# A delta-net recurrence and its feed-forward layer on one Trainium2 core: the first chunk goes from values to feed-forward by units of 128 rows, beta comes in two loads, three chunks' loads stand on two queues, and the order of all instructions is a new one

## The chip, the cores and the metric

The kernel runs on one core of one Trainium2 chip. The core has five engines, each with its own queue of instructions: PE (matmuls and transposes, with PEld for the loading of their weights), DVE (vector), ACT (activation functions and copies with a scale), POOL (a second vector engine, which also issues some DMAs) and SP (here it only issues DMAs). Engines wait for each other by semaphores. A result of PE lands in PSUM, of which there are eight banks; everything else is in SBUF.

The metric is the time of one execution on the device in microseconds (us). Before the change it was 254.03 us, the median of three runs (253.86, 254.03 and 255.42).

## The reference

Eight heads of four batches run a recurrence over 768 steps with a 48 x 48 state each. Their output, 3072 tokens of 384 numbers, goes through a feed-forward layer of width 2048.

```python
# q, k, v: [4, 8, 768, 48]   beta: [4, 8, 768]
k_n = k / (np.linalg.norm(k, axis=-1, keepdims=True) + 1e-06)
for t in range(S):
    y[:, :, t] = np.einsum('bhd,bhde->bhe', q[:, :, t], state)
    v_old = np.einsum('bhde,bhd->bhe', state, kt)
    state = state + bt[:, :, :, None] * np.einsum('bhd,bhe->bhde', kt, vt - v_old)
x = y.transpose(0, 2, 1, 3).reshape(3072, 384)
h = x @ w_in                                   # 384 x 2048
g = 0.5 * h * (1.0 + np.tanh(c * (h + 0.044715 * h * h * h)))
out = g @ w_out                                # 2048 x 384
```

## The kernel before

**Tiling.** The 768 steps are cut into 12 chunks of 64. Inside a chunk the recurrence is solved as a triangular system, so that nearly all work is matmuls; only the state goes from chunk to chunk. A chunk holds 256 tokens. It is worked on as two *units* of 128 rows (two batches x 64 steps on the 128 partitions, with the eight heads side by side); unit u belongs to chunk u // 2. Names carry the chunk or the unit: `up3.5` is block 3 of chunk 5, `B4.2` the first unit of chunk 1.

**Stages of a chunk**, with the line of the kernel before:

- *load* (L463): k, q and v, each in four DMAs of 96 KB; only chunk 0's k comes in eight of 48 KB, four for each unit (`k0x0`, `k0x1`). Chunk 0's k may be issued by ACT or SP, all others by SP.
- *norms* (L486): `sq` squares k, `sum` adds, `pow`, `eps` and `inv` give 1/(|k| + 1e-6).
- *prep* (L505): normalised k and q in bf16 (`tok`); their turned form `kT`, made either by PE transposes (`Tk`, `Tq`, `T`, all L540, and a copy) or by one DMA transpose (`turn`, SP); products of keys with keys and with queries (L564), copied as `dn` and `wq`; `vb`, the bf16 copy of v.
- *leaf* (L627): inverts the blocks on the diagonal, 8 x 8 each. `F` and `L` are matmuls, then a chain of 12 small steps follows in one of two forms: on DVE straight in PSUM (`xm`, `xa`, L655 and L658), or after a copy of the PSUM bank (`Lc`) on POOL or DVE in SBUF (`ym`, `ya`). `xb` (L669) multiplies by beta.
- *scale* (L592): `xe` spreads `xb` into the tile `zt`; `KZ` (L609) and `kz`; the scaled key products `GM` (L620); `lw` (L623).
- *invert* (L672): doubles the inverted blocks in two levels: `X10`, `X11` (affine selects, L682), then `A4`, `rt4`, `B4`, `bde4`, and `A5`, `rt5`, `B5`, `be5` (matmuls L692 and L697). The result of `B4` goes to the tile `bd` either directly (`bde40`, `bde41`) or by a copy (`xi`) and POOL (`bdc`).
- *chain* (L725): `V` (values, L759), `K` and `Q` (products with the state, L752), `R` (copy to `rs`), `U` (L773), `Un` (copy to `us`), `S` (state, L782), `Sn` (copy to `st`), `O` (output, L795), `On` (copy to `xo`), then the output is turned to `xT` by PE (`X`, L807, and the copy `xT`) or by a DMA transpose (`turnx`, L812). Chunk 0 has no state before it, so it has no `K` and `Q`.
- *mlp* (L816): 16 `up` (L824, three 256-column matmuls each), a `gelu` on ACT for each four of them (L828), 2 x 4 `down` (L835, four 384-column matmuls each), copies `Z` to `ob`, and the output DMAs.

Around these there are constants, presets of tiles, the activation-table loads `tabS` and `tabG`, the four loads of the weights on POOL's queue (`w1.0`, `w1.1`, `w2.0`, `w2.1`: half a matrix each, 768 KB in bf16; L476), beta (L428) and `fill` (L426): a 128 x 512 matmul on zeros whose result nobody reads.

**Beta.** `beta` is loaded in four DMAs: steps of chunk 0 apart from the other eleven chunks. Each part is turned (`betaT`), negated (`betaN`, four pieces), split into two bf16 summands (`betaH`, `betaL`) and spread over the partitions (`betaS`, `betaC`).

**What sets the order.** Every operation is declared once, with what it reads and writes:

```python
A(PE, op("U"), umat, reads=inv + [rbn], alloc=(ps("U"), 2), mode="m", mm=16)
A(EV, op("Un"), lambda e, P: copy(e, ub[:, :, :, :, :].rearrange("p x y g d -> p x (y g d)"), banks(P(ps("U")))),
  frees=[ps("U")], writes=[ubn])
```

Which engine executes it, in which place, in which PSUM bank and in which of its alternative forms is written in one long text, `ORDER`: `Un.0:a` puts `Un` of chunk 0 into ACT's queue at that place (p, a, d, g, s for PE, ACT, DVE, POOL, SP), `U.0@0` puts `U` on PE and its result in bank 0. An alternative that is not named there is not executed. Each engine executes its operations in just that order. The program derives the semaphore waits from the declarations, so an operation that waits holds up all that stands behind it on its engine. Chunks overlap widely: while PE does the `up` and `down` of one chunk, the other engines prepare the next two or three.

## Time and profile before

| What | Value |
|---|---|
| median of three runs | 254.03 us (253.86 to 255.42) |
| profiled execution, from its first to its last instruction | 254.7 us |
| mean granted clock of PE in it | 0.966 of full speed |
| instructions | 12256 |
| PE, busy | 226.0 us (89%), 5500 instructions |
| DVE, busy | 185.8 us (73%), 445 instructions |
| ACT, busy | 157.4 us (62%), 244 instructions |
| POOL, busy | 130.1 us (51%), 159 instructions |
| moved by DMA | 28.25 MB, mean 111 GB/s |
| `up` (L824), 576 matmuls of 128x256 | 76.8 us |
| `down` (L835), 384 matmuls of 128x384 | 72.7 us |

The profile is of one execution, by the hardware profiler. Busy times of engines overlap each other, and so do PE's matmuls and its weight loads (PEld); a share of busy time is a mean over the whole span and says nothing about one stretch of it. In rows of groups `out<-in` names the tiles, then come the operation's shape, its count, the busy time, the mean of one in ns, and the idle time of the engine just in front of them with what ended it. The granted clock is the share of its full speed at which PE was allowed to run. Records of matmuls end where a model says, so that a busy PE isn't always PE at its peak.

### The profile page before, as it was taken

To read this page: it belongs to the slowest core of one execution; us is meant where nothing else is said; L and a number is where in the kernel's file an instruction comes from. 1 tells how busy PE (TensorE), PEld (TensorE's weight loads), DVE (VectorE), ACT (ScalarE), POOL (GpSimd) and SP (SyncE) were. 2 spreads that over 40 slices of the span, in tenths; PEclk is the share of its full clock that TensorE was granted. 3 is DMA by queue.
4 is the path that set the end of the run, shared out by engine and by line. 5 is a ranking of instruction groups with operands and counts; after the bars stand their busy time and mean duration, and the time that the engine had idled before them with its cause. 6 is when DMAs were issued, how large, how long until landed. Compare 5 with 4: busy or idle time off the path is not lost.

```text
span 254.7 us, 12256 instructions
## 1 busy us (share of the span) xinstructions
PE 226.0 (89%) x5500; PEld 178.3 (70%) x5502; DVE 185.8 (73%) x445; ACT 157.4 (62%) x244; POOL 130.1 (51%) x159
## 2 busy tenths in 40 slices
...
GB/s 103 165 144 118 184 162 95 165 127 117 128 130 105 112 126 124 135 165 147 119 146 167 100 36 131 147 153 130 56 93 167 62 49 4 33 68 64 3 93 62
DMA packets 104532, 28.25 MB, mean 111 GB/s; under 512 B 98592, under 2 KB 103712, under 8 KB 104480
## 3 DMA queue, kind: packets, MB, share of 16 engines
...
q14 instruction: 9, 0.07, 0.1%
...
## 4 chain that ended last, share of the span: by engine, by line
PE 73%; DVE 15%; ACT 4%; DMA 2%; ACTq 2%; issue 2%; SPq 1%; POOL 0%
PE ps L835 24%; PE ps L824 22%; PE ps L692 5%; PE ps L620 3%; PE ps L752 3%; PE ps L773 2%; DMA vraw<-in_v_dram 2%; PE ps L697 2%; PE ps L564 2%; DVE lw L623 2%; DVE xl L658 2%; PE ps L633 2%; PE ps L759 2%; DVE ps L655 2%; PE ps L609 1%
## 5 line engine op out<-in xcount | busy, mean ns | idle before, releaser
L824 PE MATMUL ps<-xT,W 128*128 128x256 bf16 x576 | 76.8, 277 | 0.4 <-DVE xl L658 0.4
L835 PE MATMUL ps<-W,gT 128*128 128x384 bf16 x384 | 72.7, 326 | 0.0
L828 ACT ACTIVATE gT<-ps 128x1024 bf16<-128x1024 f32 x48 | 48.4, 1022 | 26.4 <-PE ps L824 25.8
L824 PEld LDWEIGHTS ps<-xT,W 128*128 128x128 bf16 x576 | 52.2, 99 | 9.3 <-DVE xl L658 0.5
L835 PEld LDWEIGHTS ps<-W,gT 128*128 128x128 bf16 x384 | 34.0, 97 | 18.2
L682 POOL TENSOR_SCALAR_AFFINE_SELECT bd<-lw 64x512 bf16<-64x512 bf16 x34 | 22.6, 667 | 37.7 <-DVE lw L623 28.6
L704 DVE TENSOR_TENSOR rl<-ps,two 128x384 bf16<-128x384 f32 (+1 forms) x48 | 22.9, 484 | 9.7 <-PE ps L692 9.5
L623 DVE CAST_PREDICATED lw<-mlw,ps 128x832 bf16<-128x832 uint16 x24 | 24.3, 1018 | 6.8 <-PE ps L620 6.5
L499 POOL TENSOR_TENSOR nrm<-nrm,half 128x16 f32<-128x16 f32 x9 | 26.6, 2956 | 2.8 <-DVE nrm L497 2.7
L343 ACT ACTIVATE bd<-ps 32x256 bf16<-32x256 f32 (+1 forms) x40 | 16.8, 428 | 8.2 <-PE ps L692 4.4
L692 PEld LDWEIGHTS ps<-lw,bd 128*128 128x128 bf16 x384 | 15.5, 98 | 4.2 <-POOL bd L682 1.2
L692 PE MATMUL ps<-lw,bd 128*128 128x32 bf16 (+1 forms) x384 | 17.2, 183 | 1.2 <-POOL bd L682 1.1
L658 DVE TENSOR_TENSOR xl<-ps,xl 128x96 bf16<-128x96 f32 (+4 forms) x72 | 16.0, 228 | 2.0
L655 DVE TENSOR_TENSOR ps<-ps,xl 128x64 f32<-128x64 f32 (+5 forms) x72 | 15.6, 221 | 2.0 <-PE ps L649 0.5
L343 ACT ACTIVATE ob<-ps 128x384 f32<-128x384 f32 x17 | 8.3, 490 | 14.0 <-PE ps L835 14.0
L722 POOL COPY bd<-xi 64x256 f32<-64x256 f32 x20 | 8.0, 401 | 16.4 <-ACT xi L343 8.5
L540 PE MATMUL ps<-ident,tok 128*128 128x128 bf16 x80 | 7.8, 246 | 8.1 <-POOL tok L531 3.8
L531 POOL TENSOR_TENSOR tok<-kraw,nrm 128x384 bf16<-128x384 f32 x9 | 8.5, 945 | 12.7 <-DVE bsb L349 5.6
L349 ACT ACTIVATE kT<-ps 128x512 bf16<-128x512 f32 x18 | 10.4, 596 | 6.4 <-PE ps L609 6.4
L343 ACT ACTIVATE dn<-ps 128x512 bf16<-128x512 f32 x18 | 10.4, 593 | 5.3 <-PE ps L564 5.3
L620 PE MATMUL ps<-kT 48*64 48x56 bf16 (+1 forms) x768 | 11.1, 196 | 2.8 <-ACT kT L349 1.4
L599 POOL TENSOR_TENSOR zt<-xb,blk 128x2048 bf16<-128x2048 bf16 x3 | 10.9, 3642 | 4.1 <-DVE xb L669 3.9
...
## 6 DMA issues: line engine op xcount, KB each, us to landing
...
W<-in_moe_w_in_dram POOLq DMA_DIRECT2D x2, 768.0 KB, 8.8
W<-in_moe_w_out_dram POOLq DMA_DIRECT2D x2, 768.0 KB, 9.6
kraw<-in_k_dram ACTq DMA_DIRECT2D x7, 48.0 KB, 3.3
...
```

The lines of the kernel that those rows point to most:

```text
L343: return e.activation(out, in_, ACT.Copy) if e is nc.scalar else e.tensor_copy(out, in_)
L499: if e is nc.scalar else e.tensor_tensor(nr[:, 1, hx], nr[:, 0, hx], half[:, hx], ALU.pow), reads=[nrn, "half"] + ["one"] * (c < ROOTS),
L620: ins = e.matmul(P(ps("GM"))[hf(a), o_ + c0:o_ + c1], kT[s][r, y, g, hf(a)], kT[s][r, z, g, C * a + c0:C * a + c1])
L623: A(("dve",), op("lw"), lambda e, P: e.copy_predicated(lw[m][:, :, 0:LW - LB], mlw[:, :, :].rearrange("p w t -> p (w t)")[:, 16:16 + LW - ...
L655: A(("dve",), f"xm{m}.{c}", lambda e, P, m=m, w=w, part=part: e.tensor_tensor(part(P), P(f"L.{c}")[:, off[m]:off[m] + 2 * H * w].rearrange ...
L658: A(("dve",), f"xa{m}.{c}", lambda e, P, m=m, part=part: e.tensor_tensor(xl[y][:, :, m + 1:LB], part(P), xl[y][:, :, m + 1:LB], ALU.add), ...
L682: A(("pool", "dve"), op(f"X1{a}"), lambda e, P, src=lw[m][hf(a), :, LW - C:LW], dst=bd[b_][hf(a), :, hf(a)], a=a: e.affine_select(out=dst, ...
L692: ins = e.matmul(P(name)[:, C * h + c0:C * h + c1], bd[b_][:, h, :], rhs[:, h, :])
L704: A(("dve",), op(f"rt{i}"), lambda e, P, i=i, c0=c0, c1=c1, r_=r_: e.tensor_tensor(r_[:, 0:H, c0:c1], P(ps(f"A{i}")).rearrange("p (h t) -> ...
L824: ins = e.matmul(P(ph)[:, 256 * f:256 * f + 256].rearrange("p (x t) -> p x t", x=2), W1[:, j, 128 * (i + f):128 * (i + f) + 128], x_[:, :, ...
L828: A(("act",), f"gelu{i // 4}.{c}", lambda e, P, i=i, ph=ph: e.activation(g_[:, i:i + 4, :], P(ph).rearrange("p (f t) -> p f t", f=4), ACT. ...
L835: ins = e.matmul(P(po)[:, 0:DM], g_[:, f, 128 * b:128 * b + 128], W2[:, f, :], start=(f == 0), stop=(f == FC - 1))
```

## The change

Five things change, and the text `ORDER` is written anew around them.

- **Chunk 0 by units.** From `V` to `xT` chunk 0 is done for each of its two units apart, on half of the columns: `Va`, `Ra`, `Ua`, `Una`, `Oa`, `Ona`, `Xa`, `xTa`, and the same with b. `S` stays whole and waits for both. Its `up` become `upa` and `upb`, 16 of three 128-column matmuls each, with a `gelua` or `gelub` for each eight of them; `down` of a unit reads the gelus of that unit alone. All other chunks stay whole.
- **Beta** comes in two DMAs instead of four, is turned by one group of 12 transposes, negated in four pieces, split once and spread by three `betaS` of four chunks each.
- **Loads**: k, q and v of chunks 0 to 2 may be issued by SP or ACT.
- **Weights**: `w1` no longer waits for chunk 1's k, `w2` no longer for chunk 0's v.
- **Order**, as counts of operations in `ORDER`, before and after: `fill` 2 and 29; units turned by PE (`T`, behind the first two chunks) 6 and 2, by `turn` 14 and 18; chunks whose output is turned by PE 4 and 1 (chunk 0, in halves), by `turnx` 8 and 11; chunks whose leaf chain runs in SBUF (`Lc`, `ym`, `ya`) none and six (0, 5, 7, 8, 9, 11); `bdc` by way of `xi` 24 (for 12 units) and none. `bde4` is then always direct, on ACT or DVE.

```diff
 ORDER (its first lines)
-bdz3:d tmplz:g k0x1.10:a k1.01:s tmpl0:g tmpl1:g bdz5:d k0x1.00:a beta11:s blk1:g ...
...
         def load_beta():
             bv = beta.rearrange("b h s -> (b h) s").rearrange("r (c t) -> r c t", t=C)
-            for z, c0, c1 in (("0", 0, 1), ("1", 1, NC)):
+            for y in range(2):
+                A(("sp", "act"), f"beta{y}", lambda e, P, y=y: e.dma_start(braw[:, :, y, :], bv), writes=[f"braw{y}"], dma="beta")
+            def trans(e, P):
+                for c in range(NC):
+                    ins = e.transpose(P("psb")[:, 32 * c:32 * c + 32], braw[:, c, :, :].rearrange("r x t -> r (x t)"), identf[:, :])
+                return ins
...
+            for i in range(NC // 4):
+                d0, d1, w = 4 * i, 4 * i + 4, 8 * H
...
+                A(PE, f"betaS{i}", own_, reads=["rows", "bh", "bl"], alloc=(f"bc{i}", 1), mode="m", mm=2 * LB)
...
         def load(c):
-                            A(("sp", "act") if c == 0 and n == "k" else SP, f"{n}{c}" + ("" if x is None else f"x{x}") + f".{a}{y}",
+                            A(("sp", "act") if c < 3 else SP, f"{n}{c}" + ("" if x is None else f"x{x}") + f".{a}{y}",
...
                 A(("pool",), f"w1.{i}", lambda e, P, f0=f0: e.dma_start(W1[:, :, f0:f0 + FF // 2], w1v[:, :, f0:f0 + FF // 2]),
-                  reads=["kraw10", "kraw11"], writes=[f"W1{i}"], dma=f"w1{i}")
+                  writes=[f"W1{i}"], dma=f"w1{i}")
                 A(("pool",), f"w2.{i}", lambda e, P, n0=n0: e.dma_start(W2[:, n0:n0 + FC // 2, :], w2v[:, n0:n0 + FC // 2, :]),
-                  reads=["vraw00", "vraw01"], writes=[f"W2{i}"], dma=f"w2{i}")
+                  writes=[f"W2{i}"], dma=f"w2{i}")
...
         def chain(c):
+            if first:
+                for x, n_ in enumerate("ab"):
...
+                    A(PE, pn("V"), vh, reads=[f"zt{us_[x] % NN}", vrn[x]], alloc=(pn("K"), 1), mode="m", mm=8)
+                    A(EV, pn("R"), lambda e, P, x=x, half=half: copy(e, rb[:, :, x, :, :].rearrange("p y g d -> p y (g d)"), half(P, "K")), frees=[pn("K")], writes=[f"{rbn}{x}"])
...
+                    A(PE, pn("U"), uh, reads=inv[2 * x:2 * x + 2] + [f"{rbn}{x}"], alloc=(pn("U"), 1), mode="m", mm=8)
...
+                    A(PE, pn("O"), oh, reads=[f"{ubn}{x}", f"wq{ss[x]}"], alloc=(pn("O"), 2), mode="t", mm=16)
...
+                    A(PE, pn("X"), xh, reads=[f"{xbn}{x}", "ident"], alloc=(pn("X"), 1), mode="m", mm=3)
+                    A(EV, pn("xT"), lambda e, P, x=x, pn=pn: copy(e, xT[0][:, x, :, :].rearrange("p j t -> p (j t)"), P(pn("X")).bitcast(BF16)[:, 0:DM]),
+                      frees=[pn("X")], writes=[f"xT0{x}"])
...
         def mlp(c):
+            if c == 0:
+                for x, n_ in enumerate("ab"):
+                    for i in range(0, FC, 8):
...
+                                for j in range(J):
+                                    ins = e.matmul(P(ph)[:, 128 * f:128 * f + 128], W1[:, j, 128 * (i + f):128 * (i + f) + 128], x_[:, x, j, :], start=(j == 0), stop=(j == J - 1))
...
+                        A(("act",), f"gelu{n_}{i // 8}.{c}", lambda e, P, i=i, ph=ph, x=x: e.activation(
+                            g_[:, i:i + 8, 128 * x:128 * x + 128], P(ph).rearrange("p (f t) -> p f t", f=8), ACT.Gelu_apprx_tanh),
...
-                    A(PE, f"down{b}{i // 4}.{c}", down, reads=[f"{gn}.{i // 4}", f"W2{i // 8}"],
+                    A(PE, f"down{b}{i // 4}.{c}", down, reads=[f"{gn}.{i // 4}.{b}", f"W2{i // 8}"],
```

Three places show how the new order stands against the old one. A row is a run of like instructions of one engine: its line, operation, tiles, shape and count.

The first place is the start of ACT's queue. `kraw` and `qraw` are the tiles that the loads fill, `one<-one` is the instruction that loads an activation table, `sq` is the square of k. Before:

```order
L472 DMA kraw<-in_k_dram 64x4x48 x2
L432 DMA braw<-in_beta_dram 32x11x64
L472 DMA kraw<-in_k_dram 64x4x48
L432 DMA braw<-in_beta_dram 32x64
L472 DMA kraw<-in_k_dram 64x4x48
L343 ACT_TABLE_LOAD
L343 ACTIVATE lw<-tmpl 128x896
L472 DMA kraw<-in_k_dram 64x4x48
L366 ACT_TABLE_LOAD
L366 ACTIVATE one<-one 128x1
L495 ACTIVATE sq<-kraw 128x384
L472 DMA kraw<-in_k_dram 64x4x48
```

and of the change:

```order
L471 DMA kraw<-in_k_dram 64x8x48
L471 DMA kraw<-in_k_dram 64x4x48 x4
L471 DMA kraw<-in_k_dram 64x8x48
L368 ACT_TABLE_LOAD
L368 ACTIVATE one<-one 128x1
L381 ACTIVATE two<-tmpl 128x64
L471 DMA kraw<-in_k_dram 64x8x48
L494 ACTIVATE sq<-kraw 128x384
```

All of chunk 0's k loads that ACT issues (the 64x4x48 ones) now stand ahead of its table load; before, one of them stood behind the first `sq`, and one more further back. The loads of beta have left this queue, and three of the 64x8x48 loads of chunks 1 and 2 are here.

The second place is ACT's queue in front of chunk 0's inversion, whose first copies are the `bd<-ps 64x8x64`. Before:

```order
L349 ACTIVATE bc<-ps 128x512
L349 ACTIVATE kT<-ps 128x2x4x64 x3
L343 ACTIVATE vb<-vraw 128x384
L343 ACTIVATE bd<-ps 64x8x64
L346 ACTIVATE bd<-ps,low 128x8x64
L343 ACTIVATE bd<-ps 64x8x64
L346 ACTIVATE bd<-ps,low 128x8x64
L343 ACTIVATE rs<-ps 128x768
```

and of the change:

```order
L351 ACTIVATE kT<-ps 128x2x4x64
L494 ACTIVATE sq<-kraw 128x768
L345 ACTIVATE vb<-vraw 128x768
L345 ACTIVATE bd<-ps 64x8x64
L345 ACTIVATE wq<-ps 128x512
L348 ACTIVATE bd<-ps,low 128x8x64
L345 ACTIVATE bd<-ps 64x8x64
L348 ACTIVATE bd<-ps,low 128x8x64
L345 ACTIVATE rs<-ps 128x2x192
```

The square of chunk 3's k (`sq<-kraw`) and the copy of v for both units (`vb<-vraw 128x768`) now stand ahead of the first `bd` copy; before, the square of chunk 3's k stood behind all of the copies shown. `rs`, the copy behind `V`, is now that of one unit.

The third place is PE's queue from chunk 0's `U` to its first `up`. Lines of the kernel before: L692 `A4` or `B4`, L773 `U`, L609 `KZ`, L795 `O`, L782 `S`, L807 `X`, L620 `GM`, L426 `fill`, L824 `up`. Before, with eight rows of L620 left out at the dots:

```order
L773 MATMUL ps<-rs,bd 128x48 x16
L609 MATMUL ps<-zt,tok 64x64 x16
L795 MATMUL ps<-us,wq 64x48 x32
L692 MATMUL ps<-lw,bd 128x32 x8
L782 MATMUL ps<-us,tok 64x48 x32
...
L807 MATMUL ps<-ident,xo 128x128 x6
L692 MATMUL ps<-rl_0,bd 128x64 x8
L426 MATMUL ps<-wz 128x512
L609 MATMUL ps<-zt,tok 64x64 x16
L824 MATMUL ps<-xT,W 128x256 x18
```

and of the change (L779 `U`, L690 `A4` or `B4`, L788 `O`, L821 `S`, L797 `X`, L608 `KZ`, L867 `upa` and `upb`):

```order
L779 MATMUL ps<-rs,bd 128x48 x16
L690 MATMUL ps<-lw,bd 128x48 x8
L788 MATMUL ps<-us,wq 64x48 x32
L821 MATMUL ps<-us,tok 64x48 x32
L690 MATMUL ps<-lw,bd 128x32 x8
L690 MATMUL ps<-rl_0,bd 128x64 x8
L797 MATMUL ps<-ident,xo 128x128 x3
L608 MATMUL ps<-zt,tok 64x64 x32
L867 MATMUL ps<-xT,W 128x128 x15
L797 MATMUL ps<-ident,xo 128x128 x3
L867 MATMUL ps<-xT,W 128x128 x3
```

`X` is now in two pieces of three transposes; the second stands behind the first fifteen `up` matmuls. The key products of chunk 2 (L620) that stood between `S` and `X` are gone from here: they come behind the first `up`.

325 lines of the change are left out of this document (176 added, 149 removed).

## The prediction

> **What bounds the kernel now.** I read the page first, then the busy time by stretches, then the chain of waits in order of time, and last the timelines of ACT and SP in the first 50 us. On the page:
>
> ```profile
> span 254.7 us, 12256 instructions
> PE 226.0 (89%) x5500; PEld 178.3 (70%) x5502; DVE 185.8 (73%) x445; ACT 157.4 (62%) x244; POOL 130.1 (51%) x159
> ```
>
> PE leads, but its 89% is a mean over two very different parts. The second view is the busy time by stretches (columns: from and to, length, busy time and instruction count of PE, PEld, DVE, ACT, POOL, then the granted clock, DMA share, GB/s):
>
> ```profile
> 5.00:10.00 5.00, 1.46 (x12) 1.35 (x12) 2.49 (x7) 4.34 (x7) 3.33 (x8) 1.00 0.94 163
> 10.00:15.00 5.00, 0.61 (x4) 0.34 (x4) 4.46 (x12) 1.99 (x5) 4.09 (x7) 1.00 0.93 158
> 30.00:35.00 5.00, 2.74 (x142) 2.38 (x142) 4.48 (x9) 2.85 (x6) 0.94 (x2) 0.79 1.25 193
> 35.00:40.00 5.00, 3.25 (x128) 2.79 (x116) 4.57 (x12) 2.54 (x5) 3.95 (x8) 0.50 0.58 107
> 45.00:50.00 5.00, 4.01 (x162) 3.43 (x160) 5.00 (x8) 4.74 (x8) 1.24 (x2) 0.66 1.13 159
> 50.00:60.00 10.00, 10.00 (x147) 8.11 (x146) 5.48 (x12) 6.52 (x10) 6.06 (x5) 0.83 0.85 124
> 50.00:205.00 155.00, 152.32 (x3921) 120.14 (x3923) 123.53 (x285) 106.43 (x164) 92.50 (x89) 0.99 0.71 122
> 50.00:251.00 201.00, 198.32 (x4714) 154.85 (x4712) 143.17 (x327) 126.32 (x190) 101.03 (x97) 0.99 0.60 104
> ```
>
> From 50 to 251 us PE idles 201.0 - 198.3 = 2.7 us in all: a dense stretch, bound by PE's own work. Before 50 us PE mostly waits, and in 35 to 40 us it had half of its clock. So the time is: the moment at which the dense stretch begins, plus PE's work from there, plus what it idles or loses to a slow clock there, plus the tail. The chain in order of time (start, length, what) shows both ends of the stretch and the links in front of it:
>
> ```profile
> 33.71 0.47 PE ps L649 x6
> 34.18 0.56 PE ps L620 x24
> 34.74 0.47 PE ps L609 x24
> 35.88 0.66 PE ps L620 x26
> ...
> 44.70 0.59 PE ps L773 x16
> 45.30 0.81 ACT us L343
> ...
> 47.06 0.56 PE ps L782 x17
> 47.61 0.43 PE ps L620 x16
> 48.04 0.76 PE ps L807 x6
> 48.79 0.43 PE ps L692 x8
> ...
> 49.58 0.43 PE ps L609 x13
> 50.01 3.74 PE ps L824 x18
> ...
> 59.59 0.45 PE ps L540 x8
> ...
> 241.07 4.91 PE ps L824 x45
> 245.98 5.21 PE ps L835 x32
> 251.22 0.49 ACT ob L343
> ```
>
> The dense stretch starts with chunk 0's first `up` (L824) at 50.0 us and ends with the last `down` at 251.2 us; 3.5 us of copy, output DMA and wait follow, which the change leaves alone.
>
> **Term A, the start of the dense stretch.** First the loads of k. ACT's timeline:
>
> ```profile
> 0.80 1.39 ACTq L472 DMA_DIRECT2D kraw<-in_k_dram  x2
> 9.60 0.60 ACTq L472 DMA_DIRECT2D kraw<-in_k_dram  x1
> 13.85 0.52 ACT L495 ACTIVATE sq<-kraw 128x384 f32<-128x384 f32 x1 [1.19 <-DMA kraw<-in_k_dram]
> 38.96 0.59 ACT L343 ACTIVATE bd<-ps 64x512 bf16<-64x512 f32 x1 [2.24 <-PE ps L692]
> ```
>
> The last of chunk 0's eight k loads is issued at 9.60 us, behind ACT's table loads, and `sq` of that half starts at 13.85. After the change the eight stand in the first five places of ACT's and SP's queues. Two issues take 1.39 us, so the fifth place goes out at 0.8 + 4 x 0.69 = 3.6 us, and with 3.3 us to landing (below) the half is there at about 7: 6.7 us earlier. DVE then gets the sums of both halves and of chunk 1 nearly at once, which I charge with 0.7: **6.0 us** (bounds: 3, if other waits fill the gap, and 6.7).
>
> The same 5 to 15 us show what the second queue can't do: DMA was busy at 0.94 with 163 GB/s while both queues issued. [...]
>
> Second, the clock. The links of PE at 33.7 to 36.5 and at 47.1 to 50.0 ran at half clock; the nine quoted ones with 0.43 us or more add up to 2.16 + 2.61 = 4.8 us. At full clock they would give back between nothing and half, 2.4; eight 128-column transposes take 0.45 us in the dense part where six took 0.76 at 48.04, but part of each link is fixed latency, so I take a third, **1.6 us**. This needs the 27 added dummy matmuls (`fill`, 128x512) to hold the clock; they cost nothing where PE waits anyway (0.61 us busy of 5 in the row 10 to 15), and up to 0.2 us each where a real matmul stands behind one.
>
> Third, the halves. From U (L773, 44.70) to the first `up` chunk 0 takes 5.3 us, with three passes over 768 columns (`us` 0.81 us; `xo` and `xT` alike). A pass over 384 columns takes 0.49 (row below), so the first half saves 3 x 0.32 = 1.0 us there, about as much again because its U, O and X are half as long, and `xT` goes to DVE instead of queueing behind `st` on ACT: **1.9 us** (bounds 0.9 and 2.6).
>
> A is 6.0 + 1.6 + 1.9 = 9.5 us: the first `up` at about 40.5 us.
>
> What stands against it is new too. In ACT's order the `sq` of chunk 3 and the `vb` of chunk 0 now stand ahead of the inversion's first `bd` copy, so ACT, and with it the path, waits for chunk 3's k and chunk 0's v. The rows for that:
>
> ```profile
> 22.85 1.99 SPq L472 DMA_DIRECT2D vraw<-in_v_dram  x3
> kraw<-in_k_dram ACTq DMA_DIRECT2D x7, 48.0 KB, 3.3
> W<-in_moe_w_in_dram POOLq DMA_DIRECT2D x2, 768.0 KB, 8.8
> kT<-tok SPq DMA_TRANSPOSE x14, 3.8
> ```
>
> SP issues one load in about 0.67 us. Chunk 3's last k load is the 30th in its new order: issued at 0.8 + 29 x 0.67 = 20.3 us. The first W1 half, which no longer waits for chunk 1's k, now goes out ahead of the last of these, and a W takes 8.8 us to land; loads behind it can be as late as it is, so I expect that k at about 20.3 + 8.8 = 29 us. The `bd` copy of 38.96 us, moved by A1 and A2 (7.6 us), is due at about 31. So the cover holds by 2 us, and if DMA is later than that, every further microsecond is on the path.
>
> **Term B, PE's work behind that point.** Groups of instructions, from the view by lines (line, engine, what, count | busy us, mean ns | idle us in front and what ended it):
>
> ```profile
> L540 PE MATMUL ps<-ident,tok 128*128 128x128 bf16 x80 | 7.8, 246 | 8.1 <-POOL tok L531 3.8 <-DVE tok L531 3.3 <-ACT bc L349 0.6
> L343 ACT ACTIVATE ob<-ps 128x384 f32<-128x384 f32 x17 | 8.3, 490 | 14.0 <-PE ps L835 14.0
> L658 DVE TENSOR_TENSOR xl<-ps,xl 128x96 bf16<-128x96 f32 (+4 forms) x72 | 16.0, 228 | 2.0
> L609 PE MATMUL ps<-zt,tok 64*64 64x64 bf16 x384 | 7.1, 201 | 2.0 <-DVE zt L602 0.9 <-DVE lw L623 0.4 <-ACT gT L828 0.3
> L669 DVE TENSOR_TENSOR xb<-xl,bc 128x128 bf16<-128x128 bf16 x8 | 2.3, 290 | 0.2
> L669 POOL TENSOR_TENSOR xb<-xl,bc 128x128 bf16<-128x128 bf16 x4 | 1.7, 428 | 7.2 <-DVE xl L658 7.2
> ```
>
> The 80 transposes of k and q become 48: four units more go by DMA, 4 x 0.45 = 1.8 us (the x8 link of 59.59). Three chunks more turn their result by DMA: 18 transposes of 0.056 us, less 3 for chunk 0's second half, which now falls behind the first `up`: 0.8 us. One block of chunk 2's key products (L620) moves behind the first `up`: half of the 0.56 to 0.66 us that it takes at half clock above, 0.3 us. The halved `up` stream the same columns. B = **2.3 us**.
>
> **Term C, the clock in the dense stretch.** The first 18 `up` took 3.74 us; 45 of them take 4.91 at full clock, so 18 should take 1.96. With the clock held that is **1.7 us**.
>
> **Term D, what comes back.** The stretch can't stay as gapless as it was: the other engines get 9.5 us less of a lead. DVE is busy 123.5 of 155 us there (80%) and would be asked for nearly the same in some 150; eleven DMA transposes instead of eight carry a chunk's result, eighteen instead of fourteen a unit's k and q, each 3.8 us from issue to landing. Half a microsecond for each of the seven new ones is 3.5; the second W1 half and the first activation table add perhaps 1.5. I charge **5 us**, between 1 and 9.
>
> **Sum**: 254.7 - 9.5 - 2.3 - 1.7 + 5 = 246.2 us of span. The profiled execution stands 0.7 us over the median of the runs, 254.03, so I forecast **245.5 us** for the median.
>
> **Rivals.**
> - *Idle stays small.* PE's 2.7 us of idle grow by only 1 instead of 5: 241.5 us. For it: DVE has 20% left. Chance 0.15.
> - *DMA holds the start.* 163 GB/s was all that 16 engines gave at share 0.94. What must come in before the second half of chunk 0's `up` (five chunks of k, four of q, three of v, beta, and W1, of which 0.77 MB a half is written) is about 5.0 + 1.6 = 6.6 MB, 40 us at that rate, and the need is at 40.5 + 2.7 = 43. At the 107 GB/s of 35 to 40 us it would not be met. Then `bd`, or the W1 half, comes 3 to 5 us late, and PE, idle that long, falls to half clock again as in 35 to 40 us: 249 to 251. For it: the cover is 2 us. Against: in the trace W pushes ahead of the small loads. Chance 0.2.
> - *The dummy matmuls don't hold the clock.* A2 and C go, 3.3 us: 248.8. [...] Against them speaks the row 30 to 35: PE was busy 2.74 of 5 us in small pieces, and lost half of its clock all the same. Chance 0.08.
> - *The leaf chains become the pace: slower.* Six of twelve chunks (0, 5, 7, 8, 9, 11) leave the PSUM form of the leaf recursion (12 steps of some 0.23 us on DVE) for a copy on ACT and steps shared by DVE and POOL. POOL takes 0.43 us where DVE takes 0.29 for the same `xb`, and each change of engine is a wait. With a 0.6 us copy, some 0.15 us for each step on POOL and 0.1 for each handover a chain is about 2 us longer. If `xb` is what PE waits for in each of the six, 12 us come back: 257.5. It decides only if `xb` reaches its chunk's KZ late; today PE idles only 2.0 us in front of the matmuls that read it (L609), 0.9 of it for `zt`. Chance 0.07.
> - *The change doesn't do what it says.* The first `up` is early, but chunk 0's stretch is then as thin as before, because chunk 1 isn't ready, and the gain is idle again: 253. Chance 0.05.
>
> **How the numbers follow.** The forecast (243 to 248) has 0.45, the rivals 0.15, 0.2, 0.08, 0.07 and 0.05. The range 241 to 250.5 leaves out the slower case, the last one, and the far ends of the first two. Faster by over 1% (below 251.5; 1% is about what a measurement here can tell from no change): 0.45 + 0.15 + 0.2 + 0.08 = 0.88; within 1%: 0.05; slower: 0.07.
>
> **What will show it.** A1: `sq` of chunk 0's second half at 7 to 8 us. A: the first `up` between 38 and 43 us. The clock: no half clock between 15 us and the end. B: 48 transposes of L539 instead of 80. D: idle in the dense stretch of 4 to 9 us, ended mostly by DMA transposes, DVE and the weights. The forecast is wrong if ACT sits before `bd` for a DMA beyond 32 us, if PE drops to half clock after 40, or if PE's idle ends at `xb`'s readers.

## The result and the profile after

The changed kernel took 265.4 us, the median of four runs (264.32 to 268.47), against 254.72 us for the kernel before beside it (253.86 to 256.76). The ratio is 1.040, with a 95% interval of 1.033 to 1.047: it became slower by 4%, where 245.5 us were forecast. Here and in all runs below, the ratio leaves out executions that took over 1.5% more than the shortest of their kernel (up to half of them), the median does not, and the profiled executions of e9, e13 and e16 were such long ones. The page of the changed kernel, its lines on the span, the engines, the queue that carries the instructions themselves, and the chain that ended last:

```profile
span 263.8 us, 12236 instructions
PE 233.3 (88%) x5506; PEld 179.6 (68%) x5511; DVE 184.3 (70%) x422; ACT 156.4 (59%) x251; POOL 122.9 (47%) x159
q8 instruction: 43, 0.70, 1.1%
PE 58%; SPq 13%; DMA 9%; DVE 6%; POOL 6%; issue 4%; ACT 2%; POOLq 0%
```

The busy time by stretches (length, busy time and count of PE, PEld, DVE, ACT and POOL, granted clock, DMA share, GB/s):

```profile
30.00:35.00 5.00, 3.41 (x84) 2.99 (x87) 4.56 (x12) 2.95 (x6) 4.08 (x10) 0.59 0.90 159
35.00:40.00 5.00, 4.16 (x104) 3.60 (x105) 3.81 (x14) 4.23 (x10) 3.50 (x5) 0.73 0.88 127
45.00:50.00 5.00, 4.53 (x103) 4.23 (x91) 2.53 (x5) 3.60 (x6) 3.52 (x2) 0.71 0.84 128
50.00:60.00 10.00, 8.29 (x217) 6.93 (x218) 7.68 (x14) 6.11 (x9) 9.76 (x12) 1.00 0.68 87
50.00:205.00 155.00, 140.95 (x3684) 110.72 (x3684) 124.11 (x272) 95.34 (x147) 80.81 (x88) 0.98 0.76 127
45.00:260.00 215.00, 200.28 (x4757) 156.13 (x4745) 148.59 (x322) 126.26 (x190) 92.93 (x97) 0.98 0.61 106
```

The dense stretch is no longer dense. It now runs from 45 to 260 us, and in it PE idles 215.0 - 200.3 = 14.7 us, where it was 2.7. These rows account for the whole difference of the two spans: the stretch starts 4.9 us earlier (50.0 to 45.1), idles 12.0 more, and is busy 2.0 more (198.3 to 200.3); 12.0 + 2.0 - 4.9 = 9.1 = 263.8 - 254.7. By the medians the loss is larger, 10.7 us: the profiled execution of the kernel before was itself some 2 us over its median (a run takes 1.8 us longer than its span, so 254.7 of span is a run of 256.5).

What PE waits for in it is in PE's timeline (start, busy, what, and in brackets the idle time before it with what ended it):

```profile
44.03 0.21 PE L690 MATMUL ps<-rl,bd 128*128 128x64 bf16 x1 [1.39 <-issue]
45.06 1.78 PE L867 MATMUL ps<-xT,W 128*128 128x128 bf16 x15
51.18 1.57 PE L867 MATMUL ps<-xT,W 128*128 128x128 bf16 x22 [1.65 <-issue]
67.06 0.34 PE L821 MATMUL ps<-us,tok 64*64 64x48 bf16 x18 [1.67 <-issue]
79.60 0.49 PE L879 MATMUL ps<-xT,W 128*128 128x256 bf16 x3 [0.74 <-issue]
108.00 0.50 PE L879 MATMUL ps<-xT,W 128*128 128x256 bf16 x3 [2.74 <-DMA xT<-xo]
120.98 0.21 PE L690 MATMUL ps<-lw,bd 128*128 128x32 bf16 x2 [0.85 <-issue]
138.56 0.42 PE L563 MATMUL ps<-kT 48*64 48x128 bf16 x16 [1.45 <-DMA kT<-tok]
152.20 0.43 PE L834 MATMUL ps<-us,wq 64*64 64x48 bf16 x30 [0.74 <-issue]
182.44 0.41 PE L695 MATMUL ps<-bd,rl 128*128 128x64 bf16 x8 [1.00 <-DVE rl L702]
```

and the larger of the two stops without a releaser that the kernel before has in its stretch:

```profile
141.24 0.50 PE L620 MATMUL ps<-kT 48*64 48x56 bf16 x39 [0.73 <-issue]
```

The largest group is one that the prediction does not know: stops that end with "issue", for which the profile has no releaser. Many fall inside a group of like matmuls: the eighth of eight L690 at 44.03, two of eight at 120.98. No semaphore stands there. In the change eleven such stops behind the first `up` add up to 8.0 us (before: two, 0.9 us); the waits with a releaser add up to 6.4 us (before 1.7).

In the trace's list of DMA packets these stops have a partner. The 43 packets of queue q8 carry 16 KB each. Those next to five of the stops, from the trace:

```
packet of q8, start and end      PE goes on    later by
41.71 - 42.64                    44.03         1.4
48.34 - 49.71                    51.18         1.5
64.39 - 65.67                    67.06         1.4
77.24 - 78.12                    79.60         1.5
before: 139.00 - 139.96          141.24        1.3
```

The trace has 11,017 records of PE and its weight loads; divided by 43 that is about 256 to a packet, and the stops in the change lie 252 to 255 records apart or a multiple of it. So the reading was, before e3 gave the size exactly: PE fetches its instructions in blocks of 256, and at some borders it has used up one block before the next is there.

### The profile page after: what moved, and what is told of

It reads as the page before. It is cut to its first block, busy times and chain, and to the rows that moved or that the text cites. A ratio compares the mean times of both kernels' runs of the same rounds, so it can differ in the third digit from the quotient of the medians.

```text
span 263.8 us, 12236 instructions
## 1 busy us (share of the span) xinstructions
PE 233.3 (88%) x5506; PEld 179.6 (68%) x5511; DVE 184.3 (70%) x422; ACT 156.4 (59%) x251; POOL 122.9 (47%) x159
## 4 chain that ended last, share of the span: by engine, by line
PE 58%; SPq 13%; DMA 9%; DVE 6%; POOL 6%; issue 4%; ACT 2%; POOLq 0%
PE ps L890 20%; PE ps L879 18%; SPq L471 13%; DMA vraw<-in_v_dram 4%; PE ps L690 4%; PE ps L750 3%; DMA xT<-xo 2%; DMA kT<-tok 2%; PE ps L695 2%; PE ps L619 2%; PE ps L757 2%; PE ps L812 2%; PE ps L563 1%; PE ps L834 1%; DMA qraw<-in_q_dram 1%
## 5 line engine op out<-in xcount | busy, mean ns | idle before, releaser
L879 PE MATMUL ps<-xT,W 128*128 128x256 bf16 x528 | 66.6, 275 | 4.1 <-DMA xT<-xo 2.7
L345 ACT ACTIVATE bd<-ps 32x256 bf16<-32x256 f32 (+1 forms) x50 | 22.5, 456 | 20.2 <-PE ps L695 8.7
L345 DVE COPY ob<-ps 128x384 f32<-128x384 f32 x12 | 6.6, 552 | 22.5 <-PE ps L890 22.3
L690 PE MATMUL ps<-lw,bd 128*128 128x32 bf16 (+1 forms) x384 | 17.5, 183 | 2.6 <-issue 1.2
L690 PEld LDWEIGHTS ps<-lw,bd 128*128 128x128 bf16 x384 | 15.4, 99 | 5.4 <-issue 1.7
L345 ACT ACTIVATE xo<-ps 128x768 bf16<-128x768 f32 (+1 forms) x13 | 9.9, 761 | 9.6 <-PE ps L834 9.6
L345 ACT ACTIVATE us<-ps 128x768 bf16<-128x768 f32 (+1 forms) x12 | 9.0, 756 | 9.8 <-PE ps L812 9.7
L563 PE MATMUL ps<-kT 48*64 48x128 bf16 (+1 forms) x448 | 10.7, 215 | 3.4 <-DMA kT<-tok 1.5
L428 PE MATMUL ps<-wz 128*128 128x512 bf16 x24 | 9.3, 526 | 4.8 <-POOL wz L357 4.8
L570 DVE CAST_PREDICATED wq<-muq,ps 128x512 bf16<-128x512 uint16 x17 | 11.6, 683 | 2.7 <-ACT dn L345 2.1
L345 ACT ACTIVATE rs<-ps 128x768 bf16<-128x768 f32 (+1 forms) x10 | 7.8, 776 | 9.7 <-PE ps L750 9.0
L828 DVE TENSOR_TENSOR st<-ps,st 128x768 bf16<-128x768 f32 x10 | 9.5, 953 | 4.1 <-PE ps L821 4.1
```

What stands on the lines that cost most here:

```text
L345: return e.activation(out, in_, ACT.Copy) if e is nc.scalar else e.tensor_copy(out, in_)
L563: ins = e.matmul(o, kT[s][r, y, g, hf(a)], kT[s][r, z, g, hf(a)])
L570: return e.copy_predicated(wq[s][:, :, :].rearrange("p (x g) t -> p x g t", x=2), muq[:, :].bitcast(U16).unsqueeze(1).unsqueeze(1).to_broa ...
L690: ins = e.matmul(P(name)[:, C * h + c0:C * h + c1], bd[b_][:, h, :], rhs[:, h, :])
L879: ins = e.matmul(P(ph)[:, 256 * f:256 * f + 256].rearrange("p (x t) -> p x t", x=2), W1[:, j, 128 * (i + f):128 * (i + f) + 128], x_[:, :, ...
```

## The experiments

Every run is a ratio to the kernel before on the same chip, with its 95% interval. The other columns are from the profiled execution: first `up`, length of the stretch up to the last `down`, the sum of the stops without a releaser in it and that of the other waits, all in us.

| Kernel | median | ratio | first `up` | stretch | stops | waits |
|---|---|---|---|---|---|---|
| before | 254.7 | 1 | 49.9 | 201.2 | 0.9 | 1.7 |
| the change | 265.4 | 1.040 (1.033 to 1.047) | 45.1 | 215.2 | 8.0 | 6.4 |
| e1 before, borders moved by 128 | 263.6 | 1.036 (1.030 to 1.041) | 50.8 | 206.2 | 6.7 | 0.3 |
| e2 change, borders moved by 128 | 267.9 | 1.055 (1.050 to 1.060) | 44.1 | 216.5 | 9.6 | 6.4 |
| e4 change, one `vb` later | 265.3 | 1.042 (1.036 to 1.049) | 44.2 | 215.5 | 7.9 | 9.0 |
| e5 change, loads in another order | 265.9 | 1.041 (1.034 to 1.049) | 43.8 | 215.5 | 5.2 | 12.2 |
| e6 change, start delayed | 270.4 | 1.059 (1.050 to 1.067) | 53.0 | 212.5 | 4.5 | 8.9 |
| e7 before, start delayed | 261.4 | 1.024 (1.017 to 1.032) | 56.6 | 198.9 | 1.5 | 1.0 |
| e8 change, tiny dummies | 265.6 | 1.039 (1.030 to 1.048) | 44.6 | 217.6 | 5.6 | 9.2 |
| e9 change, v issued by ACT | 264.0 | 1.030 (1.023 to 1.038) | 44.8 | 216.5 | 9.3 | 5.8 |
| e10 change, `xT` of three chunks by PE | 261.9 | 1.022 (1.016 to 1.028) | 44.9 | 210.4 | 3.3 | 7.3 |
| e11 change, chunk 0's `up` whole | 264.2 | 1.042 (1.036 to 1.047) | 44.8 | 213.1 | 4.3 | 8.4 |
| e12 before, v issued by ACT | 256.1 | 1.008 (1.005 to 1.011) | 49.6 | 200.3 | 0.5 | 2.3 |
| e13 new start, old rest | 255.6 | 1.000 (0.996 to 1.005) | 51.4 | 201.4 | 0.3 | 1.5 |
| e14 the same, borders elsewhere | 258.5 | 1.016 (1.013 to 1.020) | 46.5 | 207.5 | 4.8 | 1.0 |
| e15 change, W1 issued later | 263.7 | 1.041 (1.035 to 1.046) | 44.2 | 211.5 | 5.6 | 7.4 |
| e16 e10 and e9 together | 263.1 | 1.021 (1.016 to 1.026) | 44.5 | 216.7 | 9.4 | 4.1 |
| e17 as e13, the shift placed earlier | 257.8 | 1.014 (1.009 to 1.019) | 51.0 | 203.8 | 3.1 | 0.9 |
| e18 as e13, the shift placed midway | 254.1 | 0.999 (0.995 to 1.003) | 47.5 | 200.5 | 0.9 | 1.4 |

### Do the borders of the instruction blocks cost time?

e1 adds 64 small matmuls (128 instructions, half a block), whose result nobody reads, to PE's queue of the kernel before, while PE waits for the first k. Nothing behind them changes but the places at which a block ends.

```diff
+            def phase(e, P):
+                for i in range(16):
+                    for p, a in ((0, 0), (1, 1), (0, 1), (1, 0)):
+                        ins = e.matmul(P("phase")[hf(p), 64 * (i % 8) + 512 * a:64 * (i % 8) + 512 * a + 64], ident[hf(a), 0:64], ident[hf(a), 64:128])
+                return ins
```

> The kernel before, with 64 small matmuls on the identity (64x64 tiles, 128 instructions of PE with their weight loads, result not read) put into a gap of 3.8 us at the start in which PE waits for tok. Nothing else changes. Theory 1 (PE runs out of instructions): in the trace of the change PE stops 13 times in the middle of a run of matmuls, each time it goes on 1.2 to 1.5 us after the end of one of the 43 instruction packets of 16 KB, and the stops are 256 instructions apart or a multiple of it; they add up to 10.4 us, against 1.3 us in the kernel before. If a block of 256 instructions is what is fetched, 128 more instructions ahead move every border by half a block. By the times that the kernel before needs for 256 instructions from such shifted borders, blocks under 4.3 us add up to 12.0 us of shortfall where they have 5.7 now. So theory 1 expects 4 to 8 us more, 258 to 263 us, and new stops with no wait of 0.5 to 1.5 us each. Theory 2 (the stops are late waits that the profile doesn't show, and the time is lost to late loads): the 128 instructions cost what they take in a gap, nothing: within 1 us of the kernel before.

PE's timeline of e1:

```profile
53.34 3.58 PE L831 MATMUL ps<-xT,W 128*128 128x256 bf16 x17 [2.27 <-issue]
100.52 1.25 PE L831 MATMUL ps<-xT,W 128*128 128x256 bf16 x10 [0.98 <-issue]
163.37 0.34 PE L759 MATMUL ps<-st,kT 48*64 48x48 bf16 x19 [0.79 <-issue]
205.97 0.40 PE L802 MATMUL ps<-us,wq 64*64 64x48 bf16 x26 [0.87 <-issue]
```

The first `up` (L831 here) starts at 50.8 instead of 49.9, yet the kernel becomes slower by 3.6%. Its stretch is 5.0 us longer, and 5.8 us of new stops stand in it. The place of the borders alone costs nearly as much as the change did (3.6% and 4.0%). The kernel before has them where they cost nearly nothing, 0.9 us.

e2 gives the changed kernel the same 64 matmuls.

> The changed kernel with the same 128 instructions of PE put in front of the transposes of beta, where PE waits. Theory 1: the old stops (PE at instruction 1468, 1724, 1980, 2236, 2492 and so on in its records) are gone and new ones stand half a block away; blocks under 4.3 us add up to 17.6 us in place of 9.5, so 4 to 8 us more than the change, 269 to 273 us. Theory 2: the stops stay at the same matmuls, and the time stays within 1 us.

The stops move by half a block and none of the old ones stays, but their sum is 9.6 us instead of 8.0, and the kernel is 2.5 us slower, less than the 4 to 8 that were expected. So a better place is not found by any shift; this order meets stops in both.

e3 measures the fetch by itself. It leaves out the whole computation: its outputs are zeros. Four stretches of 1024 small matmuls (2048 instructions each) run alone, beside loads, beside loads and W1, and beside DMA transposes; a fifth has 384 matmuls of 256 columns.

```diff
+        def burst(n, ph, reads):
+            for i in range(n):
...
+                    for g in range(8):
+                        for p, a in ((0, 0), (1, 1), (0, 1), (1, 0)):
+                            ins = e.matmul(P(nm)[hf(p), 512 * a + C * (g % 4):512 * a + C * (g % 4) + C], wz[hf(a), 0:64], wz[hf(a), 64:128])
```

> A kernel of its own that leaves the whole computation out (the output is zeros): PE runs five stretches, of 1024 small matmuls (64x64 tiles, 64 columns) each in the first four: alone; beside loads of k, q and v on SP; beside such loads and both halves of W1 on POOL's queue; beside DMA transposes; the fifth has 384 matmuls of 256 columns beside loads. Theory 1: 256 instructions of the small kind need about 1.2 to 1.5 us of PE, but the stretches advance by one block of 256 per 3 to 4.4 us, a stop between blocks; beside loads and W1 a block takes longer, 4.5 us or more; in the fifth stretch 128 matmuls take some 14 us and there is no stop. Theory 2: no stops at borders of 256 instructions; the small matmuls go through without a gap in all stretches.

PE's timeline of e3, from the first, the second and the fifth stretch:

```profile
9.77 1.92 PE L216 MATMUL ps<-wz 64*64 64x64 bf16 x128 [2.44 <-issue]
13.22 1.92 PE L216 MATMUL ps<-wz 64*64 64x64 bf16 x128 [1.53 <-issue]
16.68 1.93 PE L216 MATMUL ps<-wz 64*64 64x64 bf16 x128 [1.53 <-issue]
...
44.32 1.93 PE L216 MATMUL ps<-wz 64*64 64x64 bf16 x128 [2.35 <-issue]
48.87 1.92 PE L216 MATMUL ps<-wz 64*64 64x64 bf16 x128 [2.62 <-issue]
...
154.75 44.02 PE L258 MATMUL ps<-wz 128*128 128x256 bf16 x384 [5.61 <-DMA rawq<-in_q_dram]
```

In e3 PE stops after each 128 small matmuls, that is 256 instructions with their weight loads. A block comes every 3.45 to 3.73 us when nothing else moves (13.22 to 16.68) and mostly every 4.0 to 4.6 us beside loads (44.32 to 48.87). In the trace a packet starts 1.1 us after PE has entered the block before (about 2.0 beside loads), takes about 1 us, and PE goes on 1.2 to 1.6 us after its end. So the blocks of small matmuls, 1.92 us of work each, are followed by stops of 1.5 to 2.6 us in these rows; 256 instructions of the wide matmuls take 14.7 us (44.02 / 3), and no stop follows them. In e3 the fetch is hidden behind wide matmuls and open behind small ones.

### Is it one late load, or the clock, or the halves of chunk 0?

In the change POOL waits 6.2 us, up to 46.5, for chunk 2's v (`vbc.2`, its bf16 copy), and the first DMA transpose goes out behind that. e4 puts this copy further back in POOL's queue.

```diff
-xb.2:g Una.0:a vbc.2:g
+xb.2:g Una.0:a
...
-GM.5@6 qb.6:g
+GM.5@6 qb.6:g vbc.2:g
```

> The changed kernel with one instruction moved on POOL: the copy of chunk 2's v (vb<-vraw 128x768, 46.48 us in the trace of the change, after 6.2 us of waiting for a load that was issued at 35.0 and landed at 46.4, beside two halves of the weights) goes behind the preparation of chunk 3 (tok), which stood behind it. Theory 2 (one late load snowballs: POOL waits for v, so chunk 3's tok is late, so SP sits from 44.7 to 52.4 in front of its DMA transpose, so the loads behind it and then xT of chunk 3 at 103 to 108 us are late): SP goes on 5 to 7 us earlier, the wait of 2.7 us for xT is gone, and the kernel is 4 to 8 us faster than the change (257 to 261 us). Theory 1 alone (instructions): at most 1.5 us, 264 to 266 us, since PE's order stays as it is.

The transpose goes out at 49.8 instead of 52.4 us, and nothing is gained: POOL then waits 3.7 us for chunk 3's q.

e5 puts SP's loads of the first chunks into the order of their use; two of the moved ones:

```diff
-w1.0:g betaN01:a k4.11:s
+w1.0:g betaN01:a k3.10:s
...
-GD.0@6 kTk.3:d k3.10:s
+GD.0@6 kTk.3:d k3.01:s
```

> The changed kernel with the copy of chunk 2's v late on POOL, as in the run before, and SP's loads in the order of need: the four k loads of chunk 4 and two v loads of chunk 2 (0.6 MB) go behind q of chunk 3 and v of chunk 1. In the run before the wait of 6.2 us for v became one of 3.7 us for chunk 3's q (landed at 48.3), SP's transpose went out at 49.8 in place of 52.4, and the time was 265.3 us, the same as the change. Theory 2 (the late loads of the start set the end): q of chunk 3 lands at 44 to 45, the transpose goes out at 46 to 47, and the kernel is 3 to 6 us faster than the change (259 to 262 us). Theory 1 (instructions) and theory 3 (what the dense stretch lacks is the preparation of all later chunks, which one load doesn't bring forward): at most 1.5 us faster, 264 to 266 us.

e5 has e4's move as well. Stops fall to 5.2 us, other waits grow to 12.2, the time stays; in e4 the stops stay at 7.9 and the waits grow to 9.0. In both runs the sum of the two is 17 us, against 14.4 in the change: what one repair takes away comes back as another wait.

PE's queue is the same in the change, e4 and e5, so the borders fall at the same instructions. Yet the stop inside the 32 matmuls of L821, 1.67 us in the change, is there in e5 and not in e4. PE's timeline of e5 and then of e4:

```profile
66.80 0.34 PE L821 MATMUL ps<-us,tok 64*64 64x48 bf16 x18 [1.97 <-issue]
```

```profile
66.80 0.44 PE L821 MATMUL ps<-us,tok 64*64 64x48 bf16 x32
```

In e4 the packet that PE needs there had ended at 64.36 us, 2.4 us before PE came to the group; in e5 it ended at 65.47. So in these two runs the border cost time where PE reached it before its packet had ended (64.83 in e5, 1.97 us of stop up to 66.80, 1.3 us behind the packet's end), and none where PE came 2.4 us behind that end; the place of the border alone did not decide.

e8 keeps all dummy matmuls, each with 16 columns instead of 512.

```diff
-                A(PE, n, lambda e, P, n=n: e.matmul(P(n), wz[:, 0:128], wz[:, :]), ...
+                A(PE, n, lambda e, P, n=n: e.matmul(P(n)[:, 0:16], wz[:, 0:128], wz[:, 0:16]), ...
```

> The changed kernel with its 29 dummy matmuls cut from 512 to 16 columns: as many instructions, hardly any time. If they hold PE's clock as the prediction had it (terms A2 and C, 3.3 us), the clock falls in the start and the kernel is 1 to 3.3 us slower than the change. Rival: they don't hold it (the granted clock was 0.59 to 0.73 between 30 and 50 us with them in place), and the time is within 1 us of the change, or a little less.

The same time and a first `up` at 44.6 us: the wide dummies hold nothing that matters.

e11 gives chunk 0 its whole `up` and gelus back (from `V` to `xT` it stays in halves), with 48 small matmuls at the start, as many as the whole `up` has fewer, so that the borders behind chunk 0 stay where they were.

```diff
-            if c == 0:
+            if c < 0:
                 for x, n_ in enumerate("ab"):
```

> The changed kernel with chunk 0's feed-forward whole again: 16 up of three 256-column matmuls behind both halves of xT, 48 matmuls (96 instructions) fewer between 45 and 60 us; 48 small matmuls at the start keep the borders of the blocks behind it where they were. Theory 1: the stops of the first 30 us of the dense stretch (1.75, 0.45, 0.47 and 1.74 us) shrink by half or more, 1 to 3 us faster than the change although its first up begins about 1 us later. By the prediction's A3 (the halves gain 1.9 us): 1 to 2 us slower.

The first `up` comes at 44.8 us, no later than with halves at 45.1, and the ratio stays. The halves from `V` to `xT` are not tested by this run.

e15 issues the first W1 half after chunk 1's scaling instead of before it.

```diff
-eps.2:d w1.0:g
+eps.2:d
...
-xe.3:d xe.2:g
+xe.3:d xe.2:g w1.0:g
```

> The changed kernel with the first half of W1 issued at about 28 us in place of 14.2 (behind the zt of POOL). In the trace of the change SP's loads take 3.3 and 2.9 us to issue while that half is on its way, chunk 3's k lands at 32.2 and ACT waits for it 2.05 us in front of the first bd copy (33.7). If the early weights hold the start back, that k lands 2 to 4 us earlier, the first bd copy is at 31 to 32 and the first up at 43 to 44; the end 0 to 2 us earlier. If the loads are bound by the bytes alone, k lands at the same time within 1 us.

ACT's timeline of e15 at the place where the change waited:

```profile
28.86 0.83 ACT L494 ACTIVATE sq<-kraw 128x768 f32<-128x768 f32 x1
31.40 0.59 ACT L345 ACTIVATE bd<-ps 64x512 bf16<-64x512 f32 x1 [0.97 <-PE ps L690]
```

Chunk 3's `sq` starts at 28.86 instead of 32.21 and the first `bd` copy at 31.40 instead of 33.69. This is the cover that the prediction feared for; its price was 2.3 us at this place. Of that, 0.9 us reaches the first `up`, and nothing that the interval can tell reaches the end.

### What is a later or earlier start worth?

e6 and e7 put 128 matmuls of 128x128 (256 instructions, so that every border behind them stays where it was; some 8 us) directly in front of chunk 0's first `up`, in the change and in the kernel before.

```diff
+            def delay(e, P):
+                for i in range(128):
+                    ins = e.matmul(P("delay")[:, 128 * (i % 4):128 * (i % 4) + 128], wz[:, 0:128], wz[:, 0:128])
+                return ins
```

> The changed kernel with 128 matmuls of 128x128 on zeros (256 instructions, so that the borders of the blocks stay where they are) directly ahead of chunk 0's first up: the dense stretch begins about 7 us later, at some 52 us. Theory 3 (the early start isn't what sets the end: chunks 3 and 4 have no more lead than before, PE reaches them early and idles): most of the 7 us is hidden in PE's idle time, 1 to 3 us slower than the change (266 to 269 us). Rival, the sum of the prediction (start, then PE's work, then a fixed idle time): 6 to 8 us slower (271 to 273 us).

> The same 128 matmuls in the kernel before, directly ahead of its first up (50.0 us). Its dense stretch idles 2.7 us in all, so both theories expect the whole 7 us, 260 to 262 us; if much less comes out, the start wasn't on its path either.

The kernel before pays 6.7 us (261.4 - 254.7), the change 5.0 us (270.4 - 265.4). The change lies between the two expectations. So an earlier start is worth most of what it gains, in either kernel. In the change the first `up` comes 7.9 us later and the stretch gives 2.7 of them back (212.5 instead of 215.2 us), with 3.5 us less of stops in it.

### How much do the DMA transposes on SP's queue cost?

e10 turns the outputs of chunks 1 to 3 by PE and a copy again, as before, instead of by `turnx`, and leaves out 18 dummies, so that the count of instructions stays about the same.

```diff
-turnx.1:s
+X.1@4 xT.1:a
...
-turnx.2:s
+X.2@5 xT.2:d
...
-turnx.3:s
+X.3@5 xT.3:a
```

> The changed kernel with the output of chunks 1 to 3 turned by PE again (six transposes and a copy each) in place of three DMA transposes, and 18 of the 29 dummy matmuls left out, so that PE executes as many instructions and the borders of the blocks behind chunk 3 stay. PE gets 1.0 us more work. Theory 4: three of SP's slowest issues (1.2 to 2.4 us each) and their 4.4 us of latency go, the wait of 2.7 us for xT at 108 us too, 1 to 4 us faster than the change. By the prediction's term B (a transpose on PE costs its time): 1 us slower.

It gives back 1.8% of the 4.0: the only single repair that shows. The stops are 3.3 us, the waits 7.3. By its trace the gain lies ahead of chunk 1's first `up`: that comes at 68.1 us instead of 72.4, with 0.3 us of stops between chunk 0's first `up` and it where the change has 4.1. Behind it the two kernels take nearly the same, 187.2 and 187.9 us to the last `down`. That `up` in PE's timeline of e10 and then of the change:

```profile
68.11 2.12 PE L877 MATMUL ps<-xT,W 128*128 128x256 bf16 x18
```

```profile
72.37 3.11 PE L879 MATMUL ps<-xT,W 128*128 128x256 bf16 x27
```

So its gain is mostly these stops. Whether they are gone because 18 dummies less move the borders there by 36 instructions, or because PE and the packets come at other times without three DMA transposes, it can't tell.

e9 lets ACT issue v from chunk 3 on; e12 does the same to the kernel before, and e16 adds it to e10.

```diff
-                            A(("sp", "act") if c < 3 else SP, f"{n}{c}" + ("" if x is None else f"x{x}") + f".{a}{y}",
+                            A(("sp", "act"), f"{n}{c}" + ("" if x is None else f"x{x}") + f".{a}{y}",
...
-v3.00:s
+v3.00:a
```

> The changed kernel with the 36 loads of v of chunks 3 to 11 issued by ACT in place of SP, at the same places of the order. PE's instructions and their order stay. In the trace of the change SP issues without a pause from 77 to 152 us (84 DMAs, 74 us of issuing in 75), where the kernel before has 72 in the same time and pauses; SP's issues and the DMAs behind them make 22% of the chain that ended last, 3% before. Theory 4 (SP's queue is full in the middle of the change, so loads and DMA transposes of chunks 5 to 8 come late): 23 issues of 0.68 us less in that stretch, waits of PE for xT and kT go, 4 to 8 us faster than the change (257 to 261 us). Theory 1 alone (instructions), or if the fetch stops take the place of the waits: within 1.5 us of the change.

> The kernel before with the same 36 loads on ACT, as a control: its SP has pauses and its dense stretch idles 2.7 us, so theory 4 expects no gain, within 1.5 us; ACT pays 0.6 us of queue for each load, so a little slower is possible.

> The changed kernel with both reliefs of SP: chunks 1 to 3 turned by PE (1.8 in a hundred faster than the change by itself) and v of chunks 3 to 11 on ACT (1.0 in a hundred by itself). If SP's queue is what both remove, they add up at most, 2 to 3 in a hundred faster than the change, 257 to 260 us, and SP pauses again between 77 and 152 us. If one hides the other, no better than the first alone, 260 to 262 us.

SP is short of time in the change: from 77 to 152 us it issues without a pause (84 DMAs, 74 us of issuing in 75). Relieving it gives the change 1.0% (the intervals overlap), costs the kernel before 0.8%, and on top of e10 gives nothing. A full queue of SP is part of the loss at most.

### The start apart from the rest

e13 takes the order of the change up to the first `up` (with whole `up`) and that of the kernel before behind it, with 120 small matmuls at the start. e14 has 48 of them there. The two kernels do the same work in the same order otherwise; 144 instructions tell them apart, somewhat over half a block.

```diff
-                for i in range(12):
+                for i in range(30):
                     for p, a in ((0, 0), (1, 1), (0, 1), (1, 0)):
```

> The change's program and order up to chunk 0's first up (loads, beta, weights, chunk 0 by units up to xT), and from there the order, engines and forms of the kernel before, with chunk 0's up whole. 120 small matmuls (240 instructions) stand in PE's idle time at the start, so that the borders of the blocks of 256 lie, behind the first up, about where the kernel before has them (144 instructions away from where they would fall). If the change's start is sound and its loss lies in the new order behind the first up (denser small matmuls, more DMA transposes on SP), this gains what the start gains, 4.9 us (first up at 45.2 for 50.0), less 1 to 3 us for chunks that aren't ready: 248 to 253 us, faster than both kernels. If the early start itself starves what follows, 257 us or more.

> The same with 48 small matmuls at the start in place of 120: 144 instructions fewer, all of them in PE's idle time, nothing else. Theory 1: the borders fall into the runs of small matmuls, as in the kernel before with 128 instructions more, which cost 9 us: 5 to 9 us slower than the kernel with 120. Without a role of the borders: the same time within 1 us.

In e13 the stretch has its old length, 201.4 us, and the kernel is as fast as the one before; the profiled execution, at 258.0 us, lies 2.5 us over its median, so that its first `up` may not be typical. In e14 the first `up` is early, 46.5 us, and the stretch is 6.3 us longer, 3.9 of them more stops than in the kernel before. PE's timeline of e14:

```profile
50.14 2.29 PE L885 MATMUL ps<-xT,W 128*128 128x256 bf16 x10 [1.21 <-issue]
67.71 0.26 PE L701 MATMUL ps<-bd,rl 128*128 128x64 bf16 x3 [0.88 <-issue]
100.00 0.28 PE L614 MATMUL ps<-zt,tok 64*64 64x64 bf16 x9 [0.75 <-issue]
160.55 0.28 PE L756 MATMUL ps<-st,kT 48*64 48x48 bf16 x11 [0.79 <-issue]
```

The rest of the loss thus lies behind the first `up`, in the new order or in its borders: 258.5 us with the old order and badly placed borders, 265.4 with the new one.

e17 and e18 look for a kernel that has both, the early start and the good borders. e17 has 72 of the 120 small matmuls among the first dummies, e18 has them as three groups of 24 at 26 to 33 us, each in place of a wide dummy.

```diff
+            for n in ('small0', 'small1', 'small2'):
+                A(PE, n, lambda e, P, n=n: [e.matmul(P(n)[:, 64 * (i % 8):64 * (i % 8) + 64], wz[:, 0:128], wz[:, 0:64]) for i in range(24)][-1], reads=["wz"], alloc=(n, 1), frees=[n], mode="m", mm=24)
```

> The kernel with the change's start and the order of before behind the first L867 matmul (that of the run without a shift), with 72 more small matmuls (144 instructions) among the start's dummy matmuls, in place of two wide ones, so that PE enters every later block of 256 instructions about where the kernel before does, at no cost to the start. Theory (the blocks' borders, not the start, cost it its lead): first L867 matmul at about 47, dense stretch 201 to 203, stops without a releaser behind the first up below 2 us in sum, 250 to 252 us, ratio 0.985 to 0.995. Rival (the start's gain can't be kept, whatever the borders): ratio 1.00 or more, or the start falls back to about 51 us once the instructions are added.

> The same 144 instructions as three groups of 24 matmuls of 128x64 that stand at 22 to 27 us in place of three wide dummies. Theory: as the run beside it, first L867 matmul 47, 250 to 252 us, stops behind it below 2 us in sum. Rival: where the added matmuls sit sets the time (they delay the q of chunk 0 or 1 again): first L867 matmul 50 or later, ratio 1.00 to 1.01.

The group of all `up` in e18, with its first and last start, and behind it the stops left in the stretch, in PE's timeline:

```profile
L887 PE MATMUL ps<-xT,W x576: 269/273/421, 47.5 to 242.5; 128*128 128x256 bf16 x192
```

```profile
71.87 0.37 PE L842 MATMUL ps<-us,wq 64*64 64x48 bf16 x23 [0.21 <-issue]
104.47 0.49 PE L698 MATMUL ps<-lw,bd 128*128 128x32 bf16 x10 [0.46 <-issue]
216.91 0.82 PE L898 MATMUL ps<-W,gT 128*128 128x384 bf16 x4 [0.26 <-issue]
```

e18 differs from e14 by dummies alone and is 4.3 us faster (254.1 against 258.5), the stretch 200.5 instead of 207.5 and the stops 0.9 instead of 4.8 us. Its profiled execution, 253.2 us, has both: start at 47.5, stretch 200.5. But over twelve runs it is the kernel before again, 0.999 (0.995 to 1.003), not the 250 to 252 us that were expected. The two profiles are of unlike executions: by its other runs on this chip the usual span of the kernel before is 254.5 - 1.8 = 252.7 us and that of e18 252.3, so the profile of before is 2.0 us over its usual span and that of e18 0.8 under it, which is most of the 3.2 us between them. e17 falls back to 51.0 at the start, as e13 did. ACT's timelines show where, e17 and then e18:

```profile
23.75 0.84 ACT L344 ACTIVATE tok<-qraw 128x768 bf16<-128x768 f32 x1 [5.56 <-DMA qraw<-in_q_dram]
```

```profile
18.82 0.84 ACT L344 ACTIVATE tok<-qraw 128x768 bf16<-128x768 f32 x1 [0.98 <-DMA qraw<-in_q_dram]
```

One q load, issued by ACT at 9.5 to 10 us in both, is there 5 us later in e17; e13 has the same row at 23.88. In the change, e14 and e18 it starts at 18.0 to 18.8. Why the place of 72 dummies on PE should decide that isn't settled, nor that it does: one execution of each kernel was profiled, and those of e13 and e17 took 2.5 and 2.2 us more than their medians, so the late load may belong to these executions.

## Why the prediction was wrong, step by step

- **The frame** held: the time is the start, PE's work, what it idles, and the tail. The two spans differ by just these terms.
- **The anchor** compared two unlike things: a span and the time of a run, which is 1.8 us longer (263.8 and 265.6 in the change). The profiled execution before was thus 2.4 us over the median, and not 0.7. The 0.7 us taken off is the same either way, so it cost nothing.
- **A**, the start: 4.9 us instead of 9.5. **A1**, the loads of k, was right: `sq` starts at 7.15 us where 7 to 8 was said, and at the first `bd` copy 5.3 us of its 6.0 are left (38.96 to 33.69). ACT's timeline of the change:

```profile
7.15 0.52 ACT L494 ACTIVATE sq<-kraw 128x384 f32<-128x384 f32 x1 [0.59 <-DMA kraw<-in_k_dram]
...
32.21 0.84 ACT L494 ACTIVATE sq<-kraw 128x768 f32<-128x768 f32 x1 [2.05 <-DMA kraw<-in_k_dram]
...
33.69 0.58 ACT L345 ACTIVATE bd<-ps 64x512 bf16<-64x512 f32 x1
```

- **The cover** of A failed by little: chunk 3's k was put at 29 us and the `bd` copy at 31; `sq` got it at 32.21, and `bd` came at 33.69. This is the "ACT sits before `bd` for a DMA beyond 32 us" of the prediction. e15 shows its price, 2.3 us there.
- **A2 and A3**, clock and halves: nothing. From the first `bd` copy to the first `up` it took 11.4 us (33.69 to 45.1), before 11.05 (38.96 to 50.01), 1.39 of it the stop at 44.03. The clock was 0.59 to 0.73 from 30 to 40 us and 0.71 from 45 to 50. That the 29 dummies hold the clock, which A2 and C need, no run shows: with them in place (24 have records, of 0.38 to 0.63 us each; the 0.2 us of the prediction was its author's estimate) the clock was the one above, and e8, with 16 columns in each, took the same, 265.6 us, at a mean clock of 0.955 (0.953 in the change). The third of 4.8 us that A2 took was an estimate too. e11 has its first `up` at 44.8 us with whole `up`, so the half `up` change nothing either. The halves themselves, from `U` to the first `up`, took 6.0 us (39.05 to 45.06) where the whole took 5.2 (44.70 to 49.94). Without the stop at 44.03 that would be 4.6, a gain of 0.6 us where A3 had 1.9. So the first `up` came at 45.1, not 40.5. The row of the first `U`:

```profile
39.05 0.36 PE L779 MATMUL ps<-rs,bd 128*128 128x48 bf16 x8 [0.22 <-DVE ps L653]
```

- **B**, PE's work: right. The transposes fell from 80 to 48 and from 7.8 to 4.8 us of busy time (the row below, and the one of L540 in the prediction). At 0.056 us for one, these 32 and 15 of the output are 2.6 us of PE's time.

```profile
L539 PE MATMUL ps<-ident,tok 128*128 128x128 bf16 x48 | 4.8, 243 | 0.4 <-POOL tok L523 0.3
L608 PE MATMUL ps<-zt,tok 64*64 64x64 bf16 x384 | 7.4, 201 | 1.0 <-DVE zt L598 0.3 <-DVE bd L348 0.3 <-ACT gT L883 0.2
```

- **C**, the clock of the first `up`: no. The 15 at 45.06 took 1.78 us; in e6, with 8 us of matmuls ahead of them, 15 take 1.00.
- **D**, what comes back: here the prediction failed. It had 5 us, 9 at most; the stretch grew by 14.0 us (201.2 to 215.2) although about 2.6 us of work had left it. 7.1 us of that are stops at borders of instruction blocks and 4.7 us more waits with a releaser. Somewhat under 5 us remain, which show as busy time (2.0 more, with 2.6 less of work). Much of it may be clock: twice behind 60 us PE was granted half of its clock, 1.3 to 1.4 us after the gaps that ended at 67.06 and 108.00, where the kernel before has full clock from 53.5 us on. Half of these 6.8 us, 3.4 us, is an estimate of the price. The rows, with the columns of the stretches above, of the change and then of before:

```profile
68.40:71.80 3.40, 3.40 (x43) 1.60 (x42) 2.15 (x7) 0.81 (x1) 2.56 (x2) 0.50 0.75 135
109.40:112.80 3.40, 3.40 (x50) 2.92 (x49) 1.98 (x4) 1.40 (x2) 0.71 (x2) 0.50 0.99 169
```

```profile
53.50:251.00 197.50, 194.82 (x4697) 152.35 (x4694) 141.62 (x323) 124.14 (x186) 98.06 (x95) 1.00 0.58 102
```

D counted DMA transposes and the lead of other engines, which are in the waits; a limit on how fast PE gets its own instructions was in no term, nor the half clock that stood behind two of the gaps. The trace of before had a sign of the first, the stop of 0.73 us without a releaser at 141.24 us with a packet of q8 in front of it; the prediction doesn't speak of it.
- **The rivals.** "Leaf chains, slower" had the sign and not the mechanism: L608, the reader behind `xb`, idles 1.0 us, 0.3 of it for `zt`; before it was 2.0. "DMA holds the start" happened by half and cost little; its 163 GB/s was no ceiling, since the prediction's own row of 30 to 35 us has 193. "The dummies don't hold the clock" was true: A2 and C, 3.3 us of the sum, did not come. Half clock after 40 us, which the prediction names as a sign that it is wrong, did. "The change doesn't do what it says" comes nearest: the lead was gone at chunk 1, whose first `up` is at 72.4 us (before 70.9), 6.4 us lost in 27, of which 4.1 are stops. It gave only idle for it, 253 us, since it knew no new loss.

What stays open: how much of the last 7 us (e14 to the change) is SP's full queue, single late transposes or again borders, since a repair of one brought another (e4, e5, e16); what makes some packets start later after PE enters a block than in e3 (48.34 is 4.3 us after 44.03); and how much of e18's early start is left in its usual execution.
